# Other orders in a block attention and SoLU feed-forward kernel: one bank's sum between the softmax sums, w_in sums by 1024 columns, the opening and closing pair

## The chip, the cores and the metric

One core of a Trainium2 chip runs the whole kernel. The metric is the device time of one execution in microseconds (us). The kernel before took 488.41 us as the median of three runs (487.9 to 489.84). The execution that was profiled took 488.25 us, and its trace spans 486.5 us from the first to the last instruction.

## The reference, cut to what matters

Two steps follow each other on 4608 tokens. Attention works in blocks of 64 tokens: 8 batches of 576 tokens, 8 heads of 64 columns, no look outside a block. Then comes a feed-forward layer with a SoLU (h times its own softmax) and a layer norm.

```
scores = scale * q_c @ k_c.T              # per block of 64 tokens and head
attn   = exp(scores - max) / (sum + 1e-09)
x      = attn @ v_c                       # 4608 x 512
h      = x @ w_in                         # 512 x 1024
e      = exp(h - max(h)); sm = e / (sum(e) + 1e-09)
solu   = h * sm
ln     = (solu - mean) / sqrt(var + 1e-06) * g_ln
out    = ln @ w_out                       # 1024 x 512
```

The result is float32. Both large products are therefore made from operands split into a high and a low part in the fp32r format, with three matmuls (high by low, high by high, low by high) for one product.

## The kernel before

The 4608 tokens are 36 tiles of 128. Each engine runs its instructions in the order in which the program was written: the kernel marks every one to stay in program order. TensorE (PE) multiplies, VectorE (DVE) and ScalarE (ACT) work on PSUM and SBUF, GpSimd (POOL) works on SBUF only and also issues DMAs, SyncE (SP) only issues DMAs.

The program has four stretches. An opening list written out by hand (START) loads and splits the weights and takes the first tiles. A loop over tiles 5 to 9 (line 1219) makes the first product of a tile as 24 matmuls into the bank pair `ph`. From tile 10 on (line 1299), `pair(i)` (line 1113) takes two tiles at a time. After the last pair come the remaining thirds of the second product.

A pair makes its first product by Strassen's scheme: seven products of half size, six matmuls each, into two PSUM banks in turn, `pa` and `pb`. Their order is a11 (bank a), s2 (b), s1 (a), s3 (b), then 24 matmuls of the second product of an older tile (`out1`, bank `po`), then s4 (a), a12 (b), a22 (a), then scores and values of the attention, then 24 matmuls of the second product of the next older tile (`out0`). Between them DVE empties the banks: `h_sum` (line 985) adds a bank to a half row of h, `h_out` (line 988) does the same and takes the row's maximum. A bank can be written again only when it has been read.

In front of these sums stands the softmax of two later tiles: `softmax_b` (line 415) sums a tile's exponentials on DVE, takes the reciprocal on DVE, and then normalises the exponentials by a product, for these tiles on POOL. In the pair before the change both tiles' sums and reciprocals come first on DVE, then `h_sum` of bank b after s2, then `z_bottom` (line 1038), which makes the low part z_l of out1's operand. On POOL the order is: low part of s3, the two normalisations, eight DMA issues of the older pair's turned rows (`issue(zmoves, 8)`, line 1139, which fill half of the tile z_t), the low parts of s4, a12 and a22 (`x_bottom`, line 957), and the inverse roots of the layer norm (`power`, line 1063).

The sums of blocks of w_in that Strassen's scheme needs are made on POOL during tiles 5 and 6 (`t_sum`, `t_top`, `t_bottom`, lines 871 to 903), each in two halves of 512 columns. The last one, t4, is made on PE in the first pair, with a positive and a negative unit matrix called `signs`; these two are written by ACT at the end of tile 8's turn of the loop (line 1291), into the buffer t_f that POOL's quarters of t1 used before.

Names in the profile: `z_h` and `z_l` are the second product's operand, `z_t` what they are made from, `z_b` the turned rows, `x_p`, `x_s`, `x_t` the first product's operands, `e` the exponentials of the attention, `attn_t` its turned weights, `s_sum` and `s_rinv` the softmax sums and their reciprocals, `t_w` the sums of w_in, `o_sb` the output rows.

Of the kernel before, what the change touches and what calls it, by code (L numbers as in the profile page):

```python
# [58 lines left out]
def chunk_attention_then_solu_ffn(  # L59
# [351 lines left out]
    def softmax_e(i):  # L411
        e = st[i, "e"]
        act.activation(e, e, AF.Exp, scale=SCALE)
# [387 lines left out]
    def whole(parts):  # L801
        for _ in parts:
            pass
# [64 lines left out]
    def f32(w):  # L868
        return [x.bitcast(F32) for x in w]

    def t_sum(of, less, more=()):

        for m in range(NCH2):
            f = raw_t[0][:, m]
            if of is not None:
                pool.tensor_tensor(out=f, in0=f32(of)[0][:, m], in1=f32(of)[1][:, m], op=ALU.add)
            for x in f32(less):
                pool.tensor_tensor(out=f, in0=f, in1=x[:, m], op=ALU.subtract)
            for x in f32(more):
                pool.tensor_tensor(out=f, in0=f, in1=x[:, m], op=ALU.add)  # L880

    def t_room():
        def room(dt):
# [9 lines left out]
        return rest  # L893

    def t_top(name):
        for m in range(NCH2):
            pool.tensor_copy(out=TW[name][0][:, m], in_=raw_t[0][:, m])

    def t_bottom(name):
        high, low = TW[name]  # L900
        for m in range(NCH2):
            pool.tensor_tensor(
                out=low[:, m], in0=raw_t[0][:, m], in1=high[:, m].bitcast(F32), op=ALU.subtract
            )

    signs = []

# [45 lines left out]
    def x_top(i, n):  # L953
        f, (high, low) = XO[i][n]
        act.copy(high, f)
# [29 lines left out]
    def h_sum(to, of, bank_):  # L985
        dve.tensor_tensor(out=to, in0=of, in1=bank_, op=ALU.add)
# [51 lines left out]
    def z_bottom(i, f=slice(0, NFC)):  # L1038
        zt, zh, zl = z_views(i)
        dve.tensor_tensor(  # L1040
            out=zl[:, f], in0=zt[:, f], in1=zh[:, f].bitcast(F32), op=ALU.subtract
        )
# [70 lines left out]
    def pair(i):  # L1113
        opening, closing = i == first_pair, i + 2 >= NT
        if not banks:
            whole_h.close()
            ps_b = ctx.enter_context(tc.tile_pool(name="ps_b", bufs=1, space=PSUM))
            banks.extend(ps_b.tile([P, HALF], F32, name=n) for n in ("pa", "pb"))
        a, b = banks
        h0, h1 = (work.tile([P, FF], F32, name="z") for _ in range(2))  # L1120
        HZ[i], HZ[i + 1] = h0, h1
        out1 = queue[0][0]
        softs = pending[:]
        pending.clear()
        zmoves = pair_moves(i - 2)

        for m in softs[-1:]:
            softmax_e(m)
        strassen(i, "a11", a, B11)
        act.copy(h0[:, left], a)  # L1130
        x_top(i, "s3")
        z_top(out1)
        x_bottom(i, "s3")
        for m in softs:
            whole(softmax_b(m))
        strassen(i, "s2", b, TW["t2"])
        h_sum(h0[:, right], h0[:, left], b)
        z_bottom(out1)
        issue(zmoves, 8)
        strassen(i, "s1", a, TW["t1"])  # L1140
        evict()
        strassen(i, "s3", b, TW["t3"])
        if opening:
            t_product("t4", B21, TW["t2"], 0)
        if not opening:
            spread(i - 1)
        for n in ("s4", "a12", "a22"):
            x_top(i, n)
        for m in softs:
            attn_turn(m)  # L1150
        h_sum(h1[:, left], h0[:, right], b)
        x_bottom(i, "s4")
        least1 = h_out((h1[:, left], h1[:, right]), a, None)
        dve.tensor_tensor(out=h0[:, right], in0=h0[:, right], in1=a, op=ALU.add)
        for p in range(1 if closing else 3):
            product()
            if opening and p == 1:
                t_product("t4", B21, TW["t2"], 1)
        for n in ("a12", "a22"):
            x_bottom(i, n)  # L1160
        if not opening:
            power(i - 2)
            power(i - 1)
        for m in (i + 4, i + 5):
            if m < NT:
                turn(m)
        load_some(9)
        store_rest()

        out0 = queue[0][0]  # L1170
        waits = (soon.pop(i + 2, []) + soon.pop(i + 3, []))[::-1]
        if closing:
            strassen(i, "a12", b, B21)
            least0 = h_out((h0[:, left], h0[:, left]), b, None)
        strassen(i, "s4", a, B22, waits, 6 * NCH2)
        if not closing:
            kept.append(out1)
            evict()
            z_top(out0)
        least0 = h_out((h0[:, right], h0[:, right]), a, least0 if closing else None)  # L1180
        if not closing:
            strassen(i, "a12", b, B21, waits, 3 * NCH2)
            least0 = h_out((h0[:, left], h0[:, left]), b, least0)
        strassen(i, "a22", a, TW["t4"], waits)
        pair_exp(i, 0, least0)
        least1 = h_out((h1[:, left], h1[:, left]), a, least1)
        pair_exp(i, 1, least1)
        if closing:
            return
        z_bottom(out0)  # L1190
        attention(i)
        for m in (i + 4, i + 5):
            if m < NT:
                load_v(m)
        x_pair(i + 2)
        x_sums(i + 2)
        pair_mul(i)
        pair_mul(i + 1)
        for _ in range(3):
            product()  # L1200
        kept.append(out0)
        pair_mean(i)
        spread(i)
        if i + 4 < NT:
            softmax_a(i + 4)
            softmax_e(i + 4)
            pending.append(i + 4)
        x_halves(i + 2)
        pair_mean(i + 1)
        pair_turn(i)  # L1210
        if i + 5 < NT:
            softmax_a(i + 5)
            pending.append(i + 5)
        pair_turn(i + 1)
        load_some(9)
        store_rest()

    first_pair = PAIRS
    for i in range(first, first_pair):
        order.on = i >= ORD  # L1220
        odd = i % 2 == 1
        turning = i + 1 == first_pair
        if i == first:
            z_turn(i - 1)
            load_batch(next_batch)
            next_batch += 1
        load_v(i + 3)
        z_split(queue[0][0], slice(0, NFC))
        if not odd:
            softmax_e(i + 3)  # L1230
            whole(softmax_b(i + 3))
            attn_turn(i + 3)
            x_high(i + 1)
            if i == first_pair - 4:
                t_sum(None, (), B11)
                t_top("t2")
                t_bottom("t2")
                rest_of_room()
            if i == first_pair - 2:
                for x in range(2, 4):  # L1240
                    t_quarter("t1", B12, B11, x)
        load_some(LOADS[i][0])
        whole(ffn_in(i))
        if odd:
            for m in (i + 1, i + 2):
                scores(m + 2)
                values(m)
        if turning:
            load_v(i + 4)
        whole(solu_a(i))  # L1250
        third()
        if i == first_pair - 5:
            rest_of_room = t_room()
            t_sum(B22, B12)
            t_top("t3")
            t_bottom("t3")
        if odd:
            softmax_a(i + 3)
            softmax_e(i + 3)
            if turning:  # L1260
                x_pair(i + 1)
                x_sums(i + 1)
            else:
                x_high(i + 1)
        else:
            x_low(i + 1)
        whole(solu_b(i))
        if odd:
            if turning:
                x_halves(i + 1)  # L1270
            else:
                x_low(i + 1)
            whole(softmax_b(i + 3))
            attn_turn(i + 3)
        else:
            for m in (i + 4, i + 5):
                turn(m)
        third()
        variance(i)
        if i == first_pair - 4:  # L1280
            for x in range(2):
                t_quarter("t1", B12, B11, x)
        third()
        load_some(LOADS[i][1])
        if turning:
            pair_turn(i)
        else:
            z_turn(i)
        store_rest()
        if i == first_pair - 2:  # L1290
            signs.append(work.tile([P, 2, P], F32R, name="signs", tag="t_f", bufs=1))
            act.copy(signs[0][:, 0], ident)
            act.activation(signs[0][:, 1], ident, AF.Copy, scale=-1.0)
        if odd:
            softmax_a(i + 4)
            if turning:
                pending.append(i + 4)

    for i in range(first_pair, NT, 2):
# [53 lines left out]
```

## Time and profile before

| what | value |
|---|---|
| median of three runs | 488.41 us |
| profiled execution, its span | 488.25 us, 486.5 us |
| PE busy | 456.0 us (94%), 4123 matmuls |
| DVE busy | 379.0 us (78%) |
| ACT busy | 289.9 us (60%) |
| POOL busy | 315.1 us (65%) |
| chain that ended last | PE 48%, DVE 17%, POOL 13%, ACT 8%, DMA 6% |
| mean granted clock of TensorE | 0.993 |

All instructions carry the line of one helper (L50), so the rows are told apart by tile names. A row of a timeline gives the start, the length (of all xN instructions together), the engine, the operation, output and inputs, and in brackets how long the engine stood idle before it and who released it. A matmul of 512 columns is shown with 0.39 us, but the next one starts 0.227 us later when nothing holds it. The ends of neighbours overlap, so an idle time in brackets is about 0.16 us shorter than the delay it makes.

### The profile page before, as it was taken

The page shows a single profiled execution, that of the slowest core. Times are in us where ns is not written, and L with a number is a line of the kernel's source. Part 1 is how long each engine was busy: PE and PEld are TensorE (multiplying, and loading weights), DVE is VectorE, ACT ScalarE, POOL GpSimd, SP SyncE. Part 2 cuts the span into 40 slices and gives each one's busy share as a digit, 9 for nine tenths or more (in the row PEclk, how much of TensorE's full clock was granted, in tenths as well). Part 3 has the DMA queues.
Part 4 walks back from the last instruction along what each step waited for, and adds up shares of the span by engine and source line. Part 5 has one row for each costly group of instructions (what it writes and reads, how often), then busy time and mean ns, then how long its engine had stood idle before and what let it go on. Part 6 is the DMA issues. An engine that isn't in the chain of part 4 may idle for free.

```text
span 486.5 us, 11435 instructions
## 1 busy us (share of the span) xinstructions
PE 456.0 (94%) x4123; PEld 364.3 (75%) x4123; DVE 379.0 (78%) x582; ACT 289.9 (60%) x511; POOL 315.1 (65%) x461
## 2 busy tenths in 40 slices
PE   6799999997997999999999999999999999999897
PEld 5655888875875777878787877777787878778676
DVE  2799987795948699888888988797979797956530
ACT  2675985543536475757484839393939393847451
POOL 0338458899984649585858576767767585859240
PEclk9899999998999999999999999999999999999999
DMA  9999786859593695878616866777670716142131
GB/s 239 300 226 332 127 147 154 180 138 174 102 207 72 157 156 142 154 182 159 171 50 161 167 163 146 170 159 171 142 202 24 197 28 189 43 134 68 41 108 43
DMA packets 193767, 72.06 MB, mean 148 GB/s; under 512 B 177128, under 2 KB 177648, under 8 KB 193328
## 3 DMA queue, kind: packets, MB, share of 16 engines
q1 hardware_dynamic: 186528, 58.63, 54.0%
q0 software_dynamic: 4736, 9.45, 7.7%
q10 hardware_dynamic: 2448, 3.28, 2.3%
q8 instruction: 32, 0.52, 0.5%
q14 instruction: 23, 0.19, 0.1%
HBM read 36.70 MB, written 9.44 MB: 95 GB/s over the span
## 4 chain that ended last, share of the span: by engine, by line
PE 48%; DVE 17%; POOL 13%; ACT 8%; DMA 6%; issue 4%; SPq 2%; DVEq 0%; ACTq 0%; POOLq 0%
PE po L50 21%; PE pa L50 8%; PE pb L50 7%; PE ph L50 6%; POOL x_p L50 5%; PE sx L50 3%; DVE z_b L50 3%; DVE s_sum L50 3%; ACT z L50 3%; DVE z L50 3%; PE sy L50 3%; POOL x_t L50 2%; DMA nat_z<-in_q_dram 2%; POOL x_s L50 2%; SPq L50 2%
## 5 line engine op out<-in xcount | busy, mean ns | idle before, releaser
L50 PE MATMUL po<-wo_l,z_h 128*128 128x512 f32 x280 | 111.0, 397 | 2.2 <-ACT z_h L50 2.2
L50 PE MATMUL po<-wo_h,z_l 128*128 128x512 f32 x280 | 109.8, 392 | 1.2 <-DVE z_l L50 1.2
L50 PE MATMUL po<-wo_h,z_h 128*128 128x512 f32 x280 | 109.4, 391 | 0.0
L50 POOL DMA_DIRECT2D z_t<-z_b x136 | 68.2, 509 | 13.4 <-DVE z_b L50 10.8
L50 POOL TENSOR_TENSOR x_s<-x_p 128x256 f32<-128x256 f32 x26 | 23.9, 920 | 77.2 <-ACT x_p L50 76.1
L50 ACT ACTIVATE o_sb<-po,r 128x512 f32<-128x512 f32 (+1 forms) x36 | 24.5, 681 | 68.9 <-DMA attn_t<-a_b 43.6
L50 DVE TENSOR_TENSOR z_l<-z_t,z_h 128x1024 fp32r<-128x1024 f32 (+1 forms) x36 | 50.9, 1413 | 16.8 <-ACT z_h L50 12.2
L50 PEld LDWEIGHTS po<-wo_h,z_l 128*128 128x128 f32 x280 | 52.6, 188 | 14.8 <-DVE z_l L50 3.3
L50 PEld LDWEIGHTS po<-wo_l,z_h 128*128 128x128 f32 x280 | 52.5, 188 | 13.5 <-ACT z_h L50 2.8
L50 PEld LDWEIGHTS po<-wo_h,z_h 128*128 128x128 f32 x280 | 52.6, 188 | 10.5
L50 POOL TENSOR_TENSOR x_t<-x_p,x_t 128x256 fp32r<-128x256 f32 x65 | 48.0, 747 | 12.2 <-ACT x_t L50 9.3
L50 DVE STREAM_TRANSPOSE z_b<-z 128x1024 f32<-128x1024 f32 x33 | 40.8, 1237 | 12.8 <-ACT z L50 5.2
L50 PE MATMUL pa<-wi_h,x_t 128*128 128x512 f32 x156 | 48.6, 390 | 0.6 <-DVE kT L50 0.4
L50 PE MATMUL pb<-t_w,x_t 128*128 128x512 f32 x156 | 40.9, 397 | 8.1 <-DVE z L50 7.6
L50 ACT ACTIVATE z_b<-z,h_nmax 128x1024 f32<-128x1024 f32 x26 | 29.9, 1151 | 28.7 <-DVE h_nmax L50 27.2
L50 PEld LDWEIGHTS pb<-t_w,x_t 128*128 128x128 f32 x156 | 28.3, 188 | 18.5 <-ACT eps L50 11.9
L50 ACT ACTIVATE z<-z,z_sum 128x1024 f32<-128x1024 f32 x34 | 39.1, 1150 | 3.5 <-DVE z L50 3.2
L50 ACT CAST z_h<-z_t 128x1024 fp32r<-128x1024 f32 (+1 forms) x36 | 35.1, 974 | 8.9 <-DMA z_t<-z_b 2.6
L50 POOL TENSOR_TENSOR e<-e,s_rinv 128x512 f32<-128x512 f32 x31 | 32.2, 1053 | 11.8 <-DVE s_rinv L50 11.1
L50 ACT ACTIVATE sq<-z 128x1024 bf16<-128x1024 f32 x36 | 37.6, 1045 | 2.5 <-POOL z L50 2.5
L50 DVE SCALAR_TENSOR_TENSOR z<-z,z_b 128x1024 f32<-128x1024 f32 x26 | 36.7, 1445 | 0.0
L50 PEld LDWEIGHTS pa<-wi_h,x_t 128*128 128x128 f32 x156 | 29.1, 188 | 7.3 <-issue 0.8
(141 smaller groups left out, 996.5 us busy)
## 6 DMA issues: line engine op xcount, KB each, us to landing
out_dram<-o_sb SPq DMA_DIRECT2D x35, 256.0 KB, 3.0
z_t<-z_b SPq DMA_DIRECT2D x128, 64.0 KB, 2.0
z_t<-z_b POOLq DMA_DIRECT2D x128, 64.0 KB, 2.7
q_st<-in_q_dram SPq DMA_DIRECT2D x96, 72.0 KB, 2.9
k_st<-in_k_dram SPq DMA_DIRECT2D x96, 72.0 KB, 2.7
v_sb<-in_v_dram SPq DMA_DIRECT2D x27, 256.0 KB, 4.5
w_raw<-in_moe_w_out_dram SPq DMA_DIRECT2D x4, 1024.0 KB, 7.1
attn_t<-a_b SPq DMA_DIRECT2D x60, 64.0 KB, 3.4
```

The source lines that it names most:

```text
L50: ins = make(*args, **kwargs)
```

## The change

In `t_sum`, `t_top` and `t_bottom` the loop over two halves goes: one instruction takes 1024 columns. In every pair, only the first tile's softmax sum and reciprocal stay in front of s2; `h_sum` of bank b comes next on DVE, then the second tile's sum and reciprocal, then `z_bottom`. In the opening pair the exponential comes after the copy of bank a, and the variance of tile 9 moves from the loop into the pair; `signs` moves to tile 9's turn; the softmax of tile 13 goes ahead of tile 9's turned rows. In the closing pair the low parts of s4, a12 and a22 go ahead of the eight DMA issues on POOL, and a22 is made in bank b. In the last pair but one, `z_bottom` of out0 goes ahead of the last `h_out`.

```diff
--- before.py
+++ after.py
@@ -870,14 +870,13 @@
 
     def t_sum(of, less, more=()):
 
-        for m in range(NCH2):
-            f = raw_t[0][:, m]
-            if of is not None:
-                pool.tensor_tensor(out=f, in0=f32(of)[0][:, m], in1=f32(of)[1][:, m], op=ALU.add)
-            for x in f32(less):
-                pool.tensor_tensor(out=f, in0=f, in1=x[:, m], op=ALU.subtract)
-            for x in f32(more):
-                pool.tensor_tensor(out=f, in0=f, in1=x[:, m], op=ALU.add)
+        f = raw_t[0]
+        if of is not None:
+            pool.tensor_tensor(out=f, in0=f32(of)[0], in1=f32(of)[1], op=ALU.add)
+        for x in f32(less):
+            pool.tensor_tensor(out=f, in0=f, in1=x, op=ALU.subtract)
+        for x in f32(more):
+            pool.tensor_tensor(out=f, in0=f, in1=x, op=ALU.add)
 
     def t_room():
         def room(dt):
@@ -893,15 +892,11 @@
         return rest
 
     def t_top(name):
-        for m in range(NCH2):
-            pool.tensor_copy(out=TW[name][0][:, m], in_=raw_t[0][:, m])
+        pool.tensor_copy(out=TW[name][0], in_=raw_t[0])
 
     def t_bottom(name):
         high, low = TW[name]
-        for m in range(NCH2):
-            pool.tensor_tensor(
-                out=low[:, m], in0=raw_t[0][:, m], in1=high[:, m].bitcast(F32), op=ALU.subtract
-            )
+        pool.tensor_tensor(out=low, in0=raw_t[0], in1=high.bitcast(F32), op=ALU.subtract)
 
     signs = []
 
@@ -1124,43 +1119,55 @@
         pending.clear()
         zmoves = pair_moves(i - 2)
 
-        for m in softs[-1:]:
-            softmax_e(m)
+        if not opening:
+            for m in softs[-1:]:
+                softmax_e(m)
         strassen(i, "a11", a, B11)
         act.copy(h0[:, left], a)
+        if opening:
+            for m in softs[-1:]:
+                softmax_e(m)
         x_top(i, "s3")
         z_top(out1)
         x_bottom(i, "s3")
-        for m in softs:
-            whole(softmax_b(m))
+        sums = [softmax_b(m) for m in softs]
+        for step in sums[:-1]:
+            next(step)
         strassen(i, "s2", b, TW["t2"])
         h_sum(h0[:, right], h0[:, left], b)
+        for step in sums:
+            whole(step)
         z_bottom(out1)
-        issue(zmoves, 8)
+        if not closing:
+            issue(zmoves, 8)
         strassen(i, "s1", a, TW["t1"])
         evict()
         strassen(i, "s3", b, TW["t3"])
         if opening:
             t_product("t4", B21, TW["t2"], 0)
-        if not opening:
-            spread(i - 1)
+        spread(i - 1)
         for n in ("s4", "a12", "a22"):
             x_top(i, n)
         for m in softs:
             attn_turn(m)
         h_sum(h1[:, left], h0[:, right], b)
         x_bottom(i, "s4")
+        if closing:
+            for n in ("a12", "a22"):
+                x_bottom(i, n)
+            issue(zmoves, 8)
         least1 = h_out((h1[:, left], h1[:, right]), a, None)
         dve.tensor_tensor(out=h0[:, right], in0=h0[:, right], in1=a, op=ALU.add)
         for p in range(1 if closing else 3):
             product()
             if opening and p == 1:
                 t_product("t4", B21, TW["t2"], 1)
-        for n in ("a12", "a22"):
-            x_bottom(i, n)
+        if not closing:
+            for n in ("a12", "a22"):
+                x_bottom(i, n)
         if not opening:
             power(i - 2)
-            power(i - 1)
+        power(i - 1)
         for m in (i + 4, i + 5):
             if m < NT:
                 turn(m)
@@ -1181,13 +1188,17 @@
         if not closing:
             strassen(i, "a12", b, B21, waits, 3 * NCH2)
             least0 = h_out((h0[:, left], h0[:, left]), b, least0)
-        strassen(i, "a22", a, TW["t4"], waits)
+        c = b if closing else a
+        strassen(i, "a22", c, TW["t4"], waits)
         pair_exp(i, 0, least0)
-        least1 = h_out((h1[:, left], h1[:, left]), a, least1)
+        if i + 4 == NT:
+            z_bottom(out0)
+        least1 = h_out((h1[:, left], h1[:, left]), c, least1)
         pair_exp(i, 1, least1)
         if closing:
             return
-        z_bottom(out0)
+        if i + 4 < NT:
+            z_bottom(out0)
         attention(i)
         for m in (i + 4, i + 5):
             if m < NT:
@@ -1267,6 +1278,9 @@
         whole(solu_b(i))
         if odd:
             if turning:
+                signs.append(work.tile([P, 2, P], F32R, name="signs", tag="t_f", bufs=1))
+                act.copy(signs[0][:, 0], ident)
+                act.activation(signs[0][:, 1], ident, AF.Copy, scale=-1.0)
                 x_halves(i + 1)
             else:
                 x_low(i + 1)
@@ -1276,24 +1290,23 @@
             for m in (i + 4, i + 5):
                 turn(m)
         third()
-        variance(i)
+        if not turning:
+            variance(i)
         if i == first_pair - 4:
             for x in range(2):
                 t_quarter("t1", B12, B11, x)
         third()
         load_some(LOADS[i][1])
         if turning:
+            softmax_a(i + 4)
             pair_turn(i)
         else:
             z_turn(i)
         store_rest()
-        if i == first_pair - 2:
-            signs.append(work.tile([P, 2, P], F32R, name="signs", tag="t_f", bufs=1))
-            act.copy(signs[0][:, 0], ident)
-            act.activation(signs[0][:, 1], ident, AF.Copy, scale=-1.0)
         if odd:
-            softmax_a(i + 4)
-            if turning:
+            if not turning:
+                softmax_a(i + 4)
+            else:
                 pending.append(i + 4)
 
     for i in range(first_pair, NT, 2):
```

## Rows read from the trace of the kernel before

**Rows 1.** Waits over the whole span: who waited for whom, total us, times, longest.
```profile
ACT z_b L50 <- DVE h_nmax L50: 27.2, 13, 5.7
...
PE pb L50 <- DVE z L50: 7.6, 11, 0.9
```

**Rows 2.** Timeline of PE in one pair: start, us, engine, operation, [idle before, releaser].
```profile
255.38 1.52 PE L50 MATMUL pa<-t_w,x_t 128*128 128x512 f32 x6
257.52 1.61 PE L50 MATMUL pb<-t_w,x_t 128*128 128x512 f32 x6 [0.62 <-DVE z L50]
...
259.43 0.40 PE L50 MATMUL po<-wo_h,z_l 128*128 128x512 f32 x1
```

**Rows 3.** Timeline of DVE in the same pair.
```profile
245.96 1.23 DVE L50 TENSOR_TENSOR z_l<-z_t,z_h 128x1024 fp32r<-128x1024 f32 x1
...
255.81 0.20 DVE L50 RECIPROCAL s_rinv<-s_sum 128x8 f32<-128x8 f32 x1
255.93 0.65 DVE L50 TENSOR_REDUCE s_sum<-e 128x8 f32<-128x520 f32 x1
...
256.73 0.65 DVE L50 TENSOR_TENSOR z<-z,pb 128x512 f32<-128x512 f32 x1
257.30 1.93 DVE L50 TENSOR_TENSOR z_l<-z_t,z_h 128x1024 fp32r<-128x1024 f32 x1
```

**Rows 4.** Timeline of POOL in the same pair.
```profile
256.10 2.05 POOL L50 TENSOR_TENSOR e<-e,s_rinv 128x512 f32<-128x512 f32 x2
258.08 4.01 POOL L50 DMA_DIRECT2D z_t<-z_b  x8
262.11 0.75 POOL L50 TENSOR_TENSOR x_t<-x_s,x_t 128x256 fp32r<-128x256 f32 x1
```

**Rows 5.** Timelines of DVE and of POOL where both start together.
```profile
295.35 1.22 DVE L50 SCALAR_TENSOR_TENSOR z<-z,z_b 128x1024 f32<-128x1024 f32 x1
...
295.35 1.82 POOL L50 TENSOR_TENSOR x_s<-x_p 128x256 f32<-128x256 f32 x1 [5.98 <-ACT x_p L50]
```

**Rows 6.** Timeline of POOL in the last pair but one.
```profile
427.78 1.96 POOL L50 DMA_DIRECT2D z_t<-z_b  x4 [2.10 <-issue]
```

**Rows 7.** Timeline of PE from tile 9 into the opening pair.
```profile
147.20 0.50 PE L50 MATMUL po<-wo_l,z_h 128*128 128x512 f32 x1 [2.05 <-ACT z_h L50]
...
159.19 1.65 PE L50 MATMUL pa<-t_w,x_t 128*128 128x512 f32 x6 [1.30 <-ACT z L50]
...
170.73 0.70 PE L50 MATMUL pa<-wi_h,x_t 128*128 128x512 f32 x2 [0.36 <-DVE kT L50]
```

**Rows 8.** Timeline of ACT in the same stretch.
```profile
145.56 0.30 ACT L50 CAST signs<-ident 128x128 fp32r<-128x128 f32 x1 [6.56 <-POOL t_w L50]
...
158.57 0.57 ACT L50 COPY z<-pa 128x512 f32<-128x512 f32 x1
```

**Rows 9.** Timelines of POOL and of DVE in tiles 5 and 6.
```profile
89.24 1.28 POOL L50 TENSOR_TENSOR t_w<-wi_h,wi_l 128x512 f32<-128x512 f32 x1
...
89.34 2.26 DVE L50 TENSOR_TENSOR z_l<-z_t,z_h 128x1024 fp32r<-128x1024 f32 x1 [0.81 <-ACT z_h L50]
...
104.61 4.02 POOL L50 DMA_DIRECT2D z_t<-z_b  x8
```

**Rows 10.** Timeline of PE in tile 7's first product, and what follows it.
```profile
108.32 0.47 PE L50 MATMUL ph<-wi_l,x_h 128*128 128x512 f32 x1 [0.32 <-DVE z L50]
...
114.10 0.50 PE L50 MATMUL ph<-wi_h,x_h 128*128 128x512 f32 x1 [2.56 <-DMA attn_t<-a_b]
...
119.04 0.69 PE L50 MATMUL sx<-kT,qT 64*64 64x64 f32 x32
```

**Rows 11.** Windows: stretch, its length, busy us of five engines, PEclk, DMA share, GB/s.
```profile
112.00:124.00 12.00, 9.59 (x152) 7.22 (x153) 7.42 (x9) 4.45 (x7) 11.61 (x13) 0.86 0.95 146
```

**Rows 12.** Timeline of PE in the closing pair.
```profile
450.65 0.73 PE L50 MATMUL pb<-wi_h,x_t 128*128 128x512 f32 x2 [0.55 <-POOL x_t L50]
...
453.71 0.47 PE L50 MATMUL pa<-wi_l,x_t 128*128 128x512 f32 x1 [0.94 <-DVE h_nmax L50]
```

## The prediction, made before the changed kernel was run

> **What bounds the kernel now.** I read the waits first, then the timeline of PE for gaps, then in each gap the engine named as releaser, back to what held it. PE is the bound nearly everywhere: in a pair it runs matmuls 0.227 us apart (six end 1.52 us after their start, of which the last takes 0.39 [rows 2]), and the time is won or lost in a few gaps. There are four kinds. In eleven pairs PE waits before s3 for DVE's sum of bank b, 7.6 us together [rows 1]. Around tile 9 and the opening pair it waits for z_h, for a copy of bank a and for turned keys [rows 7]. In tile 7's first product it waits for the turned attention weights [rows 10]. In the closing pair it waits twice, for a low part from POOL and for a bank that DVE has not emptied [rows 12]. The change touches each of the four.
>
> **The steady pairs.** s1 starts at 255.38, so s3 could start at 255.38 + 6 x 0.227 = 256.74. It starts at 257.52, and its six then take 1.61 instead of 1.52, since the first weights are no longer loaded ahead [rows 2]. That is 0.78 + 0.09 = 0.87 us lost. The releaser, the sum of bank b, starts at 256.73 because two softmax sums and two reciprocals precede it [rows 3]; it lasts 0.65, and PE follows 0.14 later.
>
> After the change it follows the first reciprocal, in the place that the second sum has now: 255.93. Its input, s2, has ended by then (s1 started at 255.38, right behind it). So PE is released at 255.93 + 0.65 + 0.14 = 256.72, just when it arrives. This wait goes.
>
> What is late next is z_l, the third operand of the product behind s3. DVE does the same work in another order, so z_l starts at 257.30 as before [rows 3]: sum of b to 256.50, second softmax sum to 257.18, reciprocal to 257.30 (spacings from the same rows). PE wants z_l for its third matmul at 256.74 + 1.36 + 0.45 = 258.55; today this matmul starts at 259.43 [rows 2]. If z_l keeps its 1.93 us, it ends at 259.23, the matmul stays at 259.43, and nothing is gained. If it takes the 1.23 us that it takes elsewhere in the pair [rows 3], it ends at 258.53 and the matmul starts at about 258.70: a gain of 0.73 us.
>
> So its length decides. POOL's second normalisation fills the second half of 256.10 to 258.15 [rows 4]; z_l started inside it and ended 1.1 us after it: it stood still until POOL had finished. Where both engines start at once, DVE keeps its 1.22 us and POOL's 0.75 us kind of operation takes 1.82, 1.1 more [rows 5, 4]. I read both as one rule of this chip for these operations: they exclude each other, whole instruction by whole instruction, and the first one holds. In the new order the second reciprocal starts at 257.18 and takes 0.20 [rows 3]; POOL cannot start before 257.38, and z_l starts at 257.30. z_l is first by 0.1 us, so I take 1.23. Bounds per pair: 0 and 0.87; I take 0.70. Times 11: 7.7 us (0 to 9.6).
>
> The Trainium skill, GPSIMD Engine Reference, section Key points, says that GpSimd shares its SBUF interfaces with VectorE and contends with instructions that have two SBUF inputs. It speaks against the change as far as it goes: the two still meet, and by it alone, with no word on who yields, z_l stays long and the sum would lose 7.7 us. Rows 5 decide for me.
>
> What POOL pays: the second normalisation now ends at about 258.45 + 1.02 = 259.45 instead of 258.15. The eight issues take 4.0 us (to 263.45) and the low part of s4 0.75 (to 264.2) [rows 4]. PE starts s4 22 matmuls after that third one, at 263.7, and wants this low part from the fifth matmul on, at 264.6, with its weights 0.2 earlier. Some 0.2 us are left, so I cost it at nothing; without that cover it costs one for one. The z_t moves land 1.3 us later too. Their user is ACT, which stands idle 27.2 us over 13 pairs, about 2.1 each, ahead of the next exponential [rows 1]; that covers it.
>
> **Tile 9 and the opening pair.** The product at 147.20 waited 2.05 for z_h [rows 7]. ACT was idle for 6.56 us before `signs`, which waited for POOL's sums of w_in, and z_h stood behind it [rows 8]. With `signs` in tile 9's turn, z_h can be made from 139.0 on, before PE asks for it at 145.0 (147.20 less 2.05 and the overlap of 0.16). From there to s1 lie 24 + 6 + 6 matmuls, 8.2 us, so without waits s1 starts at 153.2; it starts at 159.19 [rows 7]: 6.0 us lost. The last part is the wait of 1.30 for the copy of bank a at 158.57 [rows 8], in front of which ACT does tile 9's variance and an exponential; both move behind it. The operands between hang on the same chain behind z_h and move with it.
>
> Against this, the variance now stands on ACT ahead of the second t4 copy and of the issues for turned weights. The chain from there over DVE to the turned keys at 170.73 already makes PE wait 0.36 [rows 7]; I add 0.7 (0 to 1.3). The new order of softmax 13 and the turned rows I cost at nothing: the turned rows are used a product later. Sum: 6.0 - 0.7 = 5.3; I take 4.8, for waits that the moved chain may meet (2.5, the z_h wait alone, to 6.0).
>
> **The sums of w_in.** 18 POOL instructions become 9. A 256-column sum takes 0.75 [rows 4], a 512-column one 1.28 [rows 9], so 1024 columns take 1.28 + 2 x 0.53 = 2.34 instead of 2.56: by themselves small. But the first group fills POOL from 89.24 almost to the z_t issues at 104.61 [rows 9], and the turned weights are issued behind these. PE waits for them 2.56 us at 114.10, and its first product, 24 matmuls from 108.32 on, ends near 119.0 instead of 113.8: 5.2 us lost [rows 10]. The rest of the loss is clock: the granted clock has a mean of 0.86 in this stretch, between the levels of 2.4 and 1.2 GHz [rows 11], after PE stood idle. Five instructions saved in the first group and fewer meetings with DVE bring the issues about 2 us forward. I count 2 for the wait and 1.5 for the matmuls that then run at the full clock. In return DVE's z_l at 89.34, which starts 0.1 us after POOL's sum [rows 9], waits for a whole one of 1024 columns, about 1.06 us longer; of that 0.5 is still there at 108. Sum: 3.0 us (-1.0, if the weights land no earlier, to 4.7).
>
> **The closing pair.** The low part of a12 no longer stands behind eight issues, so the wait of 0.55 goes; a22 in bank b waits for a sum one product older, so the wait of 0.94 goes [rows 12]. With overlaps (0.16) and reloading (0.09) that is 2.0 us. The z_t moves come 4.3 us later and may hold z_h of the next tile: I take 1.7 (0.5 to 2.0). Moving z_l in the pair before trades PE's wait against the last exponential: 0 (-1 to 1).
>
> **Sum.** 7.7 + 4.8 + 3.0 + 1.7 = 17.2 us off the profiled execution's 488.25 (span 486.5 and 1.75 around it): 471.0. That execution is 0.16 under the median of the three runs, less than they differ among themselves.
>
> **Rivals.**
> A: z_l still meets the second normalisation. For it: the margin is 0.1 us. Against it: rows 5. The pairs gain nothing: 471.0 + 7.7 = 478.7.
> B: the turned weights land no earlier, since the DMA engines were 0.95 busy there [rows 11] and a z_l waits longer. Then -1.0 in place of 3.0: 475.0.
> C, slower: POOL becomes the bound of a pair. Its eight issues once show a pause of 2.10 us [rows 6]. Moved 1.3 us later, a pause in each pair puts the low part of s4 about 1.9 late: a net loss of 1.2 a pair, 13.2 in eleven, 491.9 against the 478.7 without the pairs' gain. The whole is slower from a net loss of 0.9 a pair on, a pause of some 1.8. Against it: one such pause is in the trace, the other pairs show 4.0.
> D: the waits go, but loads and moves hold PE as long elsewhere, and the change in effect does not do what it says: near 488.
>
> **How the numbers follow.** Forecast 0.56, A 0.15, B 0.13, C 0.08, D 0.04, more than forecast 0.04. The forecast's own range is 466 to 475. The range for 8 in 10 takes in A and B and leaves out C and D: 465.5 to 480. About 0.5% (2.4 us) is what a measurement tells from no change; faster 0.88, same 0.04, slower 0.08.
>
> **What would show it.** In a steady pair: no wait of PE before s3, z_l at 1.2 us, the second normalisation starting when z_l ends, s4 without a wait for POOL; a pair lasting 0.7 us less. z_l still at 1.9 shows A. Around tile 9: no wait for z_h, s1 some 6 us earlier against the 24 products before it, a longer wait for turned keys. In tile 7's first product: a clock near 1.0 and PE's wait under 1 us; if it stays, B. In the closing pair: no wait in a12 and a22. The forecast is wrong if PE's new third product matmul waits as long as s3 did, or if low parts from POOL appear as PE's releaser in the pairs.

## The result, and the profile after

The changed kernel takes 481.28 us (median of four runs, 480.32 to 482.55) where the kernel before takes 488.49 (four runs beside it). The ratio is 0.985, with a 95% interval of 0.9815 to 0.9885. That is 7.3 us faster where 17.2 were forecast, and 481.28 lies above the range of 465.5 to 480. The profiled execution took 482.55 us, with a span of 480.7 and a mean granted clock of 0.996.

The waits of the whole span (who waited for whom: us in total, times, longest) answer to [rows 1]:

```profile
ACT z_h L50 <- DMA attn_t<-a_b: 15.9, 7, 2.8
...
PEld pa L50 <- DMA attn_t<-a_b: 6.5, 8, 1.1
ACT z_b L50 <- DVE h_nmax L50: 4.3, 5, 2.4
PE pa L50 <- DMA attn_t<-a_b: 4.1, 7, 0.8
PE po L50 <- ACT z_h L50: 2.0, 2, 1.5
```

The eleven waits of PE for bank b are gone from the list (in two of these pairs s3 still starts 0.3 us late, less than the list shows). In their place PE waits in bank a for the turned attention weights, in seven pairs, and twice for z_h. The slack on which the prediction leaned is gone too: ACT's idle time ahead of the exponentials that ends with a row maximum fell from 27.2 us to 4.3, since ACT now waits for DMAs ahead of z_h (15.9 us in the first line, 1.0 before).

PE in the pair that answers to [rows 2]:

```profile
248.96 1.52 PE L50 MATMUL pa<-t_w,x_t 128*128 128x512 f32 x6
250.32 1.61 PE L50 MATMUL pb<-t_w,x_t 128*128 128x512 f32 x6
...
252.23 0.41 PE L50 MATMUL po<-wo_h,z_l 128*128 128x512 f32 x1
...
260.01 0.47 PE L50 MATMUL pa<-wi_l,x_t 128*128 128x512 f32 x1
261.12 0.50 PE L50 MATMUL pa<-wi_h,x_t 128*128 128x512 f32 x1 [0.64 <-DMA attn_t<-a_b]
...
262.48 0.69 PE L50 MATMUL sx<-kT,qT 64*64 64x64 f32 x32
```

s3 starts 1.36 us after s1 (2.14 before), and the third operand of the product behind it, z_l, holds nothing up: the gain of 0.78 us is there. But a22, whose six matmuls start at 260.01, lasts 2.47 us until the scores start. With six matmuls and no wait it takes 1.45, as it did in the kernel before:

```profile
267.15 0.39 PE L50 MATMUL pa<-wi_l,x_t 128*128 128x512 f32 x1
...
268.60 0.69 PE L50 MATMUL sx<-kT,qT 64*64 64x64 f32 x32
```

The 1.02 lost here are more than the 0.78 won. From s1 to the next s1 a pair takes 0.2 us more than before, as a mean of ten.

DVE, and then POOL, in the same pair, to be held against [rows 3, 4]:

```profile
249.39 0.20 DVE L50 RECIPROCAL s_rinv<-s_sum 128x8 f32<-128x8 f32 x1
249.51 0.65 DVE L50 TENSOR_TENSOR z<-z,pb 128x512 f32<-128x512 f32 x1
...
250.80 0.20 DVE L50 RECIPROCAL s_rinv<-s_sum 128x8 f32<-128x8 f32 x1
250.92 1.17 DVE L50 TENSOR_TENSOR z_l<-z_t,z_h 128x1024 fp32r<-128x1024 f32 x1
```
```profile
249.67 1.05 POOL L50 TENSOR_TENSOR e<-e,s_rinv 128x512 f32<-128x512 f32 x1
251.08 1.91 POOL L50 TENSOR_TENSOR e<-e,s_rinv 128x512 f32<-128x512 f32 x1 [0.36 <-DVE s_rinv L50]
252.94 4.01 POOL L50 DMA_DIRECT2D z_t<-z_b  x8
```

The turned weights' first issues in this pair, in the kernel before and in the changed one:

```profile
260.47 2.95 ACTq L50 DMA_DIRECT2D attn_t<-a_b  x4
```
```profile
253.77 2.45 ACTq L50 DMA_DIRECT2D attn_t<-a_b  x4
```

The order on DVE is the foreseen one, z_l takes 1.17 instead of 1.93, and the second normalisation pays with 1.91. It ends 4.0 us after s1's start (2.8 before), and POOL's eight issues begin there. The issues of the turned weights begin at 253.77, so the two sets now go out together; in the kernel before, POOL's issues began 2.4 us ahead of the weights' (258.08 [rows 4] and 260.47).

The DMA issues of the whole run (count, size, median us to landing), first of the kernel before, then of the changed one:

```profile
attn_t<-a_b SPq DMA_DIRECT2D x60, 64.0 KB, 3.4
```
```profile
attn_t<-a_b SPq DMA_DIRECT2D x60, 64.0 KB, 3.8
```

Tile 7, tile 9 and the opening pair on PE ([rows 10, 7]):

```profile
114.35 0.50 PE L50 MATMUL ph<-wi_h,x_h 128*128 128x512 f32 x1 [0.29 <-DMA attn_t<-a_b]
...
115.71 0.69 PE L50 MATMUL sx<-kT,qT 64*64 64x64 f32 x32
...
137.99 0.49 PE L50 MATMUL ph<-wi_h,x_h 128*128 128x512 f32 x1 [0.29 <-DMA attn_t<-a_b]
...
141.31 0.69 PE L50 MATMUL sx<-kT,qT 64*64 64x64 f32 x32
...
163.08 0.70 PE L50 MATMUL pa<-wi_h,x_t 128*128 128x512 f32 x2 [0.41 <-DVE kT L50]
```

Tile 7's scores start 3.3 us earlier, tile 9's only 1.75 (143.06 before): in tile 9's product PE picks up the turned weights piece by piece. The waits for z_h and for the copy of bank a are gone.

The closing pair: POOL and ACT, then PE (to be held against [rows 12]):

```profile
443.56 3.98 POOL L50 DMA_DIRECT2D z_t<-z_b  x8
```
```profile
449.29 1.15 ACT L50 ACTIVATE z_b<-z,h_nmax 128x1024 f32<-128x1024 f32 x1 [7.26 <-DMA z_t<-z_b]
...
451.57 1.12 ACT L50 CAST z_h<-z_t 128x512 fp32r<-128x512 f32 x2
```
```profile
452.22 0.50 PE L50 MATMUL po<-wo_l,z_h 128*128 128x512 f32 x1 [1.45 <-ACT z_h L50]
...
458.81 0.50 PE L50 MATMUL po<-wo_l,z_h 128*128 128x512 f32 x1 [0.58 <-ACT z_h L50]
```

Both waits of [rows 12] are gone. The first exponential stands still for 7.26 us: it writes into z_b, which the moves issued from 443.56 on still read. z_h stands behind it on ACT, and PE behind z_h.

### The profile page after: what moved, and what is told of

Its sections match the earlier page's. It is cut to its first block, busy times and chain, and to the rows that moved or that the text cites. A ratio compares the mean times of both kernels' runs of the same rounds, so it can differ in the third digit from the quotient of the medians.

```text
span 480.7 us, 11433 instructions
## 1 busy us (share of the span) xinstructions
PE 457.1 (95%) x4123; PEld 362.2 (75%) x4123; DVE 373.5 (78%) x582; ACT 288.5 (60%) x511; POOL 323.3 (67%) x452
## 4 chain that ended last, share of the span: by engine, by line
PE 37%; DMA 16%; SPq 14%; ACT 12%; POOL 10%; issue 6%; DVE 4%; ACTq 0%; POOLq 0%; DVEq 0%
PE po L50 17%; SPq L50 14%; DMA attn_t<-a_b 11%; PE ph L50 7%; PE pa L50 6%; POOL x_p L50 4%; PE sx L50 4%; PE sy L50 3%; ACT z L50 3%; DMA nat_z<-in_q_dram 2%; POOL x_t L50 2%; ACT x_t L50 2%; ACT sq L50 2%; DMA z_t<-z_b 2%; ACT z_h L50 2%
## 5 line engine op out<-in xcount | busy, mean ns | idle before, releaser
L50 POOL TENSOR_TENSOR x_s<-x_p 128x256 f32<-128x256 f32 x26 | 22.8, 878 | 59.9 <-ACT x_p L50 58.9
L50 ACT CAST z_h<-z_t 128x1024 fp32r<-128x1024 f32 (+1 forms) x36 | 35.0, 975 | 35.2 <-DMA attn_t<-a_b 15.9
L50 POOL TENSOR_TENSOR e<-e,s_rinv 128x512 f32<-128x512 f32 x31 | 43.1, 1391 | 16.3 <-DVE s_rinv L50 15.4
L50 DVE TENSOR_TENSOR z_l<-z_t,z_h 128x1024 fp32r<-128x1024 f32 (+1 forms) x36 | 43.2, 1199 | 13.3 <-ACT z_h L50 9.0
```

What stands on the lines that cost most here:

```text
L50: ins = make(*args, **kwargs)
```

## The experiments

In what follows a gain in us is (1 - ratio) x 488.5, with the ends of the ratio's interval in brackets.

**Each of the four parts alone, on the kernel before.** First the steady pairs: in `pair`, outside the opening one, the second sum moves behind `h_sum`.

```diff
-        for m in softs:
-            whole(softmax_b(m))
+        sums = [softmax_b(m) for m in softs]
+        for step in sums if opening else sums[:-1]:
+            whole(step) if opening else next(step)
         strassen(i, "s2", b, TW["t2"])
         h_sum(h0[:, right], h0[:, left], b)
+        for step in sums:
+            whole(step)
```

> The kernel before with one part of the change alone: in the steady pairs bank b's sum stands between the two softmax sums. Theory: PE's wait before s3 turns into a wait for turned weights in a22, the time stays: 487.5 to 490. Rival (the forecast's term): 0.7 us a pair, 480 to 482.

Measured: 490.73 us, ratio 1.0037 (1.0014 to 1.0061), so 1.8 us slower. PE's wait moved to a22, as the theory had it; the time lies 0.7 us above the theory's range. Its waits, and PE in the same pair as above:

```profile
PE pa L50 <- DMA attn_t<-a_b: 3.9, 8, 1.2
```
```profile
269.13 0.43 PE L50 MATMUL pa<-wi_l,x_t 128*128 128x512 f32 x1
270.16 0.50 PE L50 MATMUL pa<-wi_h,x_t 128*128 128x512 f32 x1 [0.61 <-DMA attn_t<-a_b]
```

Then the sums of w_in (the diff's three functions, as they stand there):

> The kernel before with the sums of w_in by 1024 columns and nothing else. Theory (the sums bring the z_t issues of tile 5 forward by some 2.3 us and PE's first product in tile 7 by 3.3, and 1.6 of this is given back in tile 9, where PE waits for turned attention weights whose moves stand behind loads of w_in's keys on the SP queue): 486.4 to 487.2, a gain of 1.3 to 2.1 us. Rival 1 (the 3.0 us of the prediction come when the part stands alone, and tile 9's waits belong to the opening edits): 485.0 to 485.8. Rival 2 (in the kernel before, tile 9's wait for z_h is set by POOL's sums and eats everything up to tile 7, then gains from the shorter sums): a gain of 4 or more.

Measured: 484.14 us, ratio 0.9918 (0.9885 to 0.995): 4.0 us faster (2.4 to 5.6). This is above the theory's 1.3 to 2.1 and rival 1's 2.6 to 3.4 and at rival 2's "4 or more". Tile 7's scores start 4.1 us earlier and tile 9's 3.3. As rival 2 has it, the wait for z_h behind tile 9 shrinks too, since `signs` gets through at 140.69 instead of 145.56 [rows 8]. The same product in the kernel before waited 2.05 [rows 7]:

```profile
142.34 0.50 PE L50 MATMUL po<-wo_l,z_h 128*128 128x512 f32 x1 [0.46 <-ACT z_h L50]
```

So s1 of the opening pair comes 4.9 us earlier, 1.6 of them behind tile 9's scores.

Then the opening pair (the diff's lines with `opening` or `turning`, nothing else):

> The kernel before with the edits of the opening pair alone: signs in tile 9's turn, tile 9's variance and the last exponential behind the copy of bank a, softmax 13 a step later, w_out's powers for both tiles of the pair. Theory (these edits are worth the 5.8 us by which s1 of the opening pair came nearer to tile 9's scores in the changed kernel, and little of it is taken back): 482.0 to 483.2. Rival (part of the 5.8 belongs to w_in's shorter sums, since signs waited for POOL's sums in the kernel before and POOL gets through these earlier): 484 to 486.

Measured: 482.71 us, ratio 0.9889 (0.9854 to 0.9924): 5.4 us faster (3.7 to 7.1), as the theory had it. From tile 9's scores to s1 of the opening pair it takes 10.3 us, where it took 16.1.

Last the closing pair (the diff's lines with `closing`, bank `c`, and the earlier `z_bottom(out0)`):

> The kernel before with the edits of the closing pair alone (and z_l one step earlier in the pair before it). Theory (two waits of together 2.0 us go, and waits for z_h of about the same come in their place): 487.6 to 488.8, no measurable change. Rival (the 1.7 us of the prediction come when the pairs ahead are as before): 486.4 to 487.2.

Measured: 489.25 us, ratio 1.0006 (0.9988 to 1.0024): no change. Its trace has the two waits for z_h, in place of those of [rows 12]:

```profile
458.80 0.50 PE L50 MATMUL po<-wo_l,z_h 128*128 128x512 f32 x1 [1.47 <-ACT z_h L50]
465.40 0.50 PE L50 MATMUL po<-wo_l,z_h 128*128 128x512 f32 x1 [0.59 <-ACT z_h L50]
```

The four add up: 4.0 + 5.4 - 1.8 - 0.3 = 7.3 us, which is what the whole change measures. That they meet to the tenth is luck: each has an interval of 0.9 to 1.7 us to either side, and the sums of w_in and the opening edits both shorten the one wait for z_h.

**The steady pairs' order undone in the changed kernel.**

```diff
-        for step in sums[:-1]:
-            next(step)
+        for step in sums if not opening else sums[:-1]:
+            whole(step)
```

> The changed kernel with one part undone: in the eleven steady pairs both softmax sums come in front of bank b's sum again. Theory: the part gained nothing, because PE's wait before s3 came back as a wait for the turned attention weights in a22 (in the trace of the changed kernel a pair takes 0.1 us more than before). So undoing it leaves the time of the changed kernel, 481.3, or about 1.2 us less: 479 to 482. In its trace the wait before s3 is back (0.6 to 0.9) and the wait in a22 is gone. Rival: the part is worth its forecast 7.7 us and the other parts fell short; then 488 to 490.

Measured: 478.68 us, just under the theory's range, ratio 0.9811 (0.978 to 0.9842), 1.9 us less than the changed kernel by the ratios, though the two intervals overlap. PE's wait for bank b is back (6.7 us, ten times), that for the weights in bank a is gone.

**The waits put where the weights are read.** The program hangs the waits for loads and moves that the next attention needs on matmuls ahead of it, one on each, from s4 on; those for the turned weights come last and fall on the last matmuls of a12 and the first of a22. The weights are read only by the values, behind the scores. Here their eight waits go to the last eight matmuls of the first scores.

```diff
+        later = [x for x in waits if x.ins.name in weights]
+        waits = [x for x in waits if x.ins.name not in weights]
...
-        attention(i)
+        attention(i, later)
...
-                    pe.matmul(
+                    ins = pe.matmul(
...
+                    at += 1
+                    if waits and 4 * HP - at < len(waits):
+                        tc.add_manual_dep(ins.ins, waits.pop().ins.name, ...)
```

> The changed kernel; in all pairs but the last two the waits of PE for the eight moves of turned weights stand on the last eight matmuls of the next scores, right in front of the values that read them, instead of on matmuls of a12 and a22; the waits for turned keys and for v slide to a22. Theory: PE stopped in a22 for data that it reads 1.5 us later, so the wait of 0.4 to 0.8 us (with restart 0.9) a pair shrinks to 0.2 or less in some nine pairs: 473 to 476. Rival: ACT is as late as the weights (z_h and the exponentials stand behind the same later moves), the copies after the values start hardly earlier, and the wait comes back before s3 or before the second product: 478 to 481.

Measured: 473.75 us, ratio 0.9706 (0.9676 to 0.9736). The theory holds. a22 runs through, 1.45 us to the scores:

```profile
255.69 0.39 PE L50 MATMUL pa<-wi_l,x_t 128*128 128x512 f32 x1
255.92 0.39 PE L50 MATMUL pa<-wi_h,x_t 128*128 128x512 f32 x1
256.15 0.39 PE L50 MATMUL pa<-wi_l,x_t 128*128 128x512 f32 x1
256.37 0.84 PE L50 MATMUL pa<-wi_h,x_t 128*128 128x512 f32 x3
257.14 0.69 PE L50 MATMUL sx<-kT,qT 64*64 64x64 f32 x32
257.66 0.65 PE L50 MATMUL sx<-attn_t,v_sb 64*64 64x64 f32 x32
```

A little of the rival is there too: in five of the eleven pairs s3 starts 0.3 to 0.4 us late again.

The same late waits on the kernel before:

> The kernel before with the late waits alone, the softmax sums in their old order. Theory (in the old order PE waits ahead of s3 for DVE, and the turned weights have landed by a22; the late wait frees nothing in the steady pairs): 486.5 to 489, at most the tile 7 and 9 waits go. Rival (the early waits cost about as much in the old order and were just not on the chain): 480 to 483, and then the late waits are a gain by themselves and the pair edit is worth little.

Measured: 487.21 us, ratio 0.9984 (0.9959 to 1.001). In the old order the late waits are worth nothing that can be told from zero, and PE still waits for bank b (7.0 us, eleven times). So the pair edit and the late waits pay only together, as far as these runs show; the two without the other parts were not run. In the late waits' kernel s3 of the first steady pair is 9.6 us ahead of the kernel before and that of the tenth after it 15.9: 0.63 us a pair, where the prediction took 0.70.

**What makes the weights late.** The same products with the moves of POOL out of the weights' way:

```diff
-        if not closing:
+        if opening:
             issue(zmoves, 8)
...
             for n in ("a12", "a22"):
                 x_bottom(i, n)
+            issue(zmoves, 8)
```

> The changed kernel, but in the steady pairs POOL issues its eight z_t moves behind the three low parts instead of ahead of them, some 2 us later, so that they meet the turned attention weights less. Theory (a22 waits for the turned weights partly because their moves now share the DMA engines with POOL's z_t moves: 3.9 us to landing instead of 3.3): landing comes back to about 3.3 us and the waits in a22 shrink from 0.4 to 0.9 to under 0.3. Rival (the weights are late only because PE comes 0.87 us earlier to a22 while they are issued 0.28 us earlier): landing and waits stay. The time itself should not gain by either: z_h and with it the two exponentials come 1.5 to 2 us later in every pair, so 481 to 487.

Measured: 495.96 us, ratio 1.0133 (1.0098 to 1.0168). On what the run was for, the theory holds. The median to landing:

```profile
attn_t<-a_b SPq DMA_DIRECT2D x60, 64.0 KB, 2.6
```

No pair waits for weights in a22, though PE reaches its second matmul 6.4 us after the first issue of the weights in this kernel as in the changed one (6.9 in the kernel before). The price was misjudged by 9 us or more: z_h now comes so late that PE waits for it in eleven places, and for z_l behind it.

```profile
PE po L50 <- ACT z_h L50: 12.0, 11, 2.4
PE po L50 <- DVE z_l L50: 4.9, 9, 0.6
```

**The closing pair.** With the eight issues back ahead of the low parts:

```diff
-        if not closing:
-            issue(zmoves, 8)
+        issue(zmoves, 8)
...
-            issue(zmoves, 8)
         least1 = h_out((h1[:, left], h1[:, right]), a, None)
```

> The changed kernel with one order undone in the closing pair: the eight issues of z_t stand in front of the low parts of s4, a12 and a22 again; a22 stays in bank b. Theory: the exponentials of the closing pair are written where the moves still read, so they waited 7.3 us for the late moves, and z_h behind them held PE for 1.45 and 0.58 us. With the moves first PE waits 0.5 to 0.8 for a12's low part again, but not for z_h: 1.5 us less, 479.3 to 480.3. Rival: z_h is late for another reason (the order of DVE and ACT in the last pairs); then 481 to 482.5, the low part's wait on top.

Measured: 478.48 us, ratio 0.9811 (0.9776 to 0.9845), somewhat better than expected, though its interval overlaps with that of the changed kernel. The wait for z_h shrinks to 0.17, and the low part of a12 is late again:

```profile
443.37 0.74 PE L50 MATMUL pb<-wi_h,x_t 128*128 128x512 f32 x2 [0.84 <-POOL x_t L50]
```

With the order of the changed kernel, but the exponentials in other tiles:

```diff
         e = turned["b"].rearrange("p q s a t -> p (q s a t)")[:, m * FF:(m + 1) * FF]
+        if i + 2 >= NT:
+            e = work.tile([P, FF], F32, name="z_e", tag="w_a", bufs=5)
```

> The changed kernel, with the closing pair's two exponentials written into tiles that are free by then (those of t3) instead of z_b, which the late z_t moves still read. Theory (the exponentials stood 7.3 us for the moves and z_h stood behind them): the first exponential starts some 4 us earlier, at 445 to 446, the wait for z_h of 1.45 falls to 0.3 or less and that of 0.58 goes: 479.0 to 480.2. Rival (z_h waits for its own moves to land, whatever the exponentials do): 480.8 to 481.6.

Measured: 478.17 us, ratio 0.9778 (0.9745 to 0.9811), 3.5 us better than the changed kernel by the ratios. ACT no longer stands for the moves, and z_h comes in time for the first of the two products; the second still waits 0.42, which the theory had going:

```profile
444.60 1.16 ACT L50 ACTIVATE z_e<-z,h_nmax 128x1024 f32<-128x1024 f32 x1 [4.56 <-DVE h_nmax L50]
...
447.34 0.62 ACT L50 CAST z_h<-z_t 128x512 fp32r<-128x512 f32 x1
```

The two waits fell by 1.6 us together; that the time fell by more is within the noise of the two ratios. So the late moves cost through the buffer they read, and at most a little through their own landing.

**Versions that beat both.** Late waits, and the closing issues first:

> The changed kernel with both mends: PE's waits for the turned attention weights on the last eight matmuls of the scores, and the closing pair's eight issues of z_t ahead of its low parts. If the two are independent their gains add: 481.3 - 7.5 - 2.8 = 471.0, so 469.5 to 472.5. Rival (with the pairs tighter, the closing pair's low parts behind the issues hold PE as long as z_h did): 473 to 475, no gain over the late waits alone.

Measured: 472.19 us, ratio 0.9671 (0.9639 to 0.9703). Late waits, exponentials in their own tiles, and the issues between the two low parts:

> The changed kernel with the late waits, the closing exponentials in their own tiles, and the closing eight issues between the low parts of a12 and a22. If the closing pair's two costs both go (z_h behind the moves, and the low part of a12 behind them): 473.75 - 1.45 - 0.56 = 471.7, within 470.0 to 472.0. Rival (the closing pair is bound by the landing of its moves): 473 to 474.

Measured: 472.64 us, ratio 0.9655 (0.9626 to 0.9684). This median falls between theory and rival: the low part of a22, behind the issues, now holds PE for 0.98.

```profile
439.72 0.72 PE L50 MATMUL pb<-wi_h,x_t 128*128 128x512 f32 x2 [0.98 <-POOL x_t L50]
```

Their intervals overlap with each other and with that of the late waits alone; each of the three is clearly faster than the changed kernel.

## Why the prediction was wrong

**The steady pairs, 7.7 forecast, -1.8 alone.** The failing step stands under "What POOL pays": "The z_t moves land 1.3 us later too. Their user is ACT ...; that covers it." It asked who uses the moves, and not what else goes out at that time. The turned weights do. They land later beside POOL's moves (3.8 instead of 3.4 us, 2.6 with the moves issued later), and PE, now 0.7 us earlier (in the pair shown a22 starts 11.05 us after s1 instead of 11.77), meets waits that the program hangs on a22, two products ahead of the reader. The prediction never looked at those waits in the pairs, though it had met the weights in tile 7.

The Trainium skill, DMA: Bandwidth & Descriptors, section Issuing engines are not separate DMA queues, says that transfers started by different engines end up on the same DMA engines and interleave. The runs agree, with the medians of 3.4, 3.8 and 2.6 us above.

The rest of that part held in the main. s3 starts at most 0.3 us late, z_l took 1.17 us for a forecast 1.23, so rival A is out, and with late waits a pair gains 0.63 us for the 0.70. Of the 0.87 us counted as lost, the 0.09 put down to weights not loaded ahead did not come back: s3's six matmuls take 1.61 without a listed wait as well. Rival C, POOL as the bound, is out for the pairs as a whole, but what it describes happens once: in the last pair but one the eight issues pause for 1.43 us, as they did in [rows 6], and PE waits 0.77 us for the low part of s4. The other ten pairs show no such wait. That the pairs end without a gain is nearest to rival D in kind ("moves hold PE as long elsewhere"), which the prediction gave 0.04 and put on the whole change instead of on the pairs.

**Tile 9 and the opening pair, 4.8 forecast, 5.4 (3.7 to 7.1) alone.** Right. The longer wait for turned keys did not come: 0.41 us instead of 0.36. Some 1.6 us of this gain would have come from the shorter sums of w_in as well, which the prediction did not count.

**The sums of w_in, 3.0 forecast, 4.0 (2.4 to 5.6) alone.** Right in the mechanism: in the changed kernel the z_t issues start at 102.28 instead of 104.61 [rows 9], PE's wait in tile 7 falls from 2.56 to 0.29, the granted clock there is 1.00 instead of 0.86 [rows 11], and z_l pays 1.09 us for a longer neighbour. Rival B is out.

```profile
102.28 4.01 POOL L50 DMA_DIRECT2D z_t<-z_b  x8
```
```profile
112.00:124.00 12.00, 11.71 (x171) 9.37 (x170) 10.95 (x14) 6.39 (x11) 11.32 (x12) 1.00 0.83 141
```

The size is in part luck: the 4.0 holds 1.6 us of the wait for z_h, which the forecast had put under tile 9. That tile 9 takes back 1.6 of tile 7's 3.3 us in the trace of the changed kernel is not explained. PE's waits for weights or values in that product differ from kernel to kernel, from nothing in the last one above to 0.95 us in the one with the late moves, and 0.63 in one that has the old sums. No run here separates the cause.

**The closing pair, 1.7 forecast, -0.3 (-1.2 to 0.6) alone.** The mechanism was named ("may hold z_h of the next tile") and mis-sized: 0.3 us was set against the 2.0, and the waits for z_h are 1.45 and 0.58. The prediction had z_h wait for its data; it waited behind an exponential that could not write its buffer.

## What to carry to other kernels

When an instruction moves by a microsecond, follow the DMA issues behind it to the transfers beside which they now run, and not only to their own reader. A wait sits where the program put it, not where the data is read: before an edit brings an engine forward, look for waits placed early on its way, and move them to the reader. A transfer that is made later also keeps the buffer that it reads for longer; look who writes there next.

## What the runs showed of the hardware

Two instructions of DVE and POOL that both read two SBUF operands take turns, whole instruction by whole instruction. In tile 5 of the changed kernel POOL's 1024-column sums and DVE's z_l meet twice, POOL first, then DVE:

```profile
89.23 2.36 POOL L50 TENSOR_TENSOR t_w<-wi_h,wi_l 128x1024 f32<-128x1024 f32 x1
91.67 3.27 POOL L50 TENSOR_TENSOR t_w<-t_w,wi_h 128x1024 f32<-128x1024 f32 x1
```
```profile
89.33 3.35 DVE L50 TENSOR_TENSOR z_l<-z_t,z_h 128x1024 fp32r<-128x1024 f32 x1 [0.87 <-ACT z_h L50]
```

z_l stands until POOL's first sum ends at 91.59 and then takes its own 1.1; the second sum stands until z_l has ended at 92.68 and then takes 2.3. The Trainium skill, SBUF — State Buffer, section SBUF: two separate sides, states such a lock, held for the whole instruction by whichever starts first; these rows and the pair's 1.17 and 1.91 agree.
